# A first stage in an order written out by hand on four engines, weights as a pipeline of half chunks, and batch 1's inputs in room that batch 0 has left

## The chip, the cores and the metric

The kernel runs on one core of one Trainium2 chip. Times are microseconds on the device. A comparison uses the median of several executions; one more execution is profiled, and all rows of a trace below come from that one. TensorE is called PE, VectorE DVE, ScalarE ACT, GpSimd POOL, and SyncE, which issues most of the DMAs, SP.

## What is computed

Three layers follow each other on 8 batches of 576 tokens with 512 channels.

```python
# attention, 8 heads of 64; keys and values are pooled 8 to 1 (72 positions)
k_p = k.reshape(B, H, 72, 8, D).mean(axis=3); v_p = likewise
attn = softmax(q @ k_p^T / 8)
x = attn @ v_p                                  # then heads side by side: (B, 576, 512)
# mixer 1: rank 32 over the tokens, then a channel MLP with 2048 hidden units
u = x + ((x^T @ U) @ V)^T
x = u + relu(u @ w_ch1) @ w_ch2
# mixer 2: real part of a 2-D FFT over tokens and channels, layer norm, channel MLP
u = x + real(fft(fft(x, axis=1), axis=2))
x = u + relu(layernorm(u) @ w_ch1b) @ w_ch2b
```

The weights and U, V arrive as float64 and are turned into float32 on the chip by integer instructions.

## The kernel before

**The long loop.** All 4608 tokens go through both channel MLPs in blocks of 256 tokens. `groups` lists them: the first group takes blocks 0 and 1 together (`wide`), then one block at a time, first for mixer 1, then for mixer 2. In a group a loop runs over the NF = 16 chunks f of 128 hidden units: `st1` makes the hidden chunk (names `h<-uth,w` and `h<-utl,w`), ACT and DVE split it into a high and a low part (`hh`, `hl`, and for odd f of the wide group `hw`; lines 666 and 667), and `st2`, one or two steps later, multiplies it with the second weight (`o`, `h`, `m` `<-w,hh`, `<-w,hl`, `<-w,hw`). Every float32 product is made of three products of high and low parts. Between these, `lanes` (generators stepped by `step`) do the attention of the next batches (`a`), the token mixing (`mix`), the pooling of keys and values (`prep`), the weights (`w`), and later the FFT.

**The first stage.** Before that loop can begin, batch 0 has to pass attention and token mixing. `Attn.prep` loads k and v of a batch (`kT`, `vr`) and pools them on DVE (`kp` L267, `vp` L270). `tile_steps` takes one of five tiles of up to 128 tokens through: scores (`s<-k,q`), the maximum (L334), eight exponentials (L337), transposes (L341, L342), their copy to SBUF (L345, L346), the product with v (`<-v,e`), the division (L358), and the split into `xh` and `xl` (`split`, L98 and L92). `hu_mm` sums the tiles into `hu`. When all five are in, `mix_split` makes `hst` of it, `mix_mm` mixes (`<-hst,vst`) and adds (L95), and `block_prep` transposes and splits into `uth` and `utl` what the loop reads.

**Weights.** A half chunk (weight k of chunk f) is a DMA of 512 KB into `wraw`, then a shift on DVE (L116), an Abs on ACT in place (L117), two bit operations on DVE (L121, L122), a copy on ACT that rounds to the high part (L98), and a subtraction on POOL (L92) for the low part. `w_first` does this for the first weights, both halves of a chunk in one step. Chunks wait in SBUF rooms that are also `scratch` rooms: `scratch(i)` lies where the weight chunk 15 - i // 2 will lie.

**Order.** A scheduler orders the instructions of each engine, from its own model of their times, by priority; `urgent()` raises that of the attention of batch 0. SP's DMAs are issued in one order too, and their packets share the same 16 DMA engines.

Of the kernel before, what the change touches and what calls it, by code (L numbers as in the profile page):

```python
# [8 lines left out]
F32 = mybir.dt.float32  # L9
# [24 lines left out]
GROUPS = ((0,), (1, 2), (3, 4, 5), (6, 7))  # L34
F64_BIAS = float.fromhex("0x1p-112")
# [3 lines left out]
def kernel(  # L39
# [30 lines left out]
    state = {"n": 0, "free": False, "m": "s1", "u": 0, "slot": 0, "x1": 0, "u2": 0}  # L70
# [33 lines left out]
    def urgent():  # L104

        return tc.high_priority(offset=4000)

# [21 lines left out]
    def w_first(tmp):  # L129
        raws, ts = {}, {}  # L130

        def loads(upto):
            while len(raws) < min(NF, upto) and (len(raws) < (NF - 1 if state["free"] else 5) or NF - 2 in ts):
# [4 lines left out]
        def done(f):  # L138
            for k in range(2):
                w = wp.tile([128, 2, 512], F32R, tag=f"w{k}_{f}", name="w")  # L140
                W[k, f] = w
                split(w[:, 0], w[:, 1], ts[f][k].bitcast(F32), nc.gpsimd)
        loads(2)
        yield
        for f in range(NF + 1):
            loads(f + 3)
            while len(raws) < min(NF, f + 1):
                yield
                loads(f + 3)
            if f == NF - 1:  # L150
                done(f - 1)
            if f < NF:
                if f < NF - 2:
                    t = scratch(f % 2)
                    t = [t[:, 512 * k:512 * k + 512].bitcast(I32) for k in range(2)]
                else:
                    t = [tmp().bitcast(I32) for k in range(2)]
                ts[f] = t
                for k in range(2):
                    high(raws[f][k], 512, t[k])  # L160
            yield
            if f and f != NF - 1:
                done(f - 1)
            if f < NF:
                for k in range(2):
                    bits(raws[f][k], 512, t[k])
                yield
# [30 lines left out]
    class Attn:  # L198
# [44 lines left out]
        def prep(self, b):  # L243
# [5 lines left out]
            def load(i):  # L249
                t = scratch(2 + i) if b == 0 else self.tmp()  # L250
# [6 lines left out]
            ahead = 9 if b == 0 else 2  # L257
# [55 lines left out]
        def tile_steps(self, b, t, alt=0, before=None):  # L313
# [11 lines left out]
            if before:  # L325
                before()
            sf = scratch(3 + alt) if alt else p1.tile([128, S], F32, tag="s", name="s")
# [423 lines left out]

    lanes = {}
    at_pool = []

    abx = ExitStack()
    at = Attn(abx)
    at_pool.append(at.p)
# [230 lines left out]
```

## Time and profile before

| | us |
|---|---|
| median of 3 runs (1990.57 to 1992.56) | 1991.53 |
| the profiled execution, its own time | 1994.14 |
| its span, first to last instruction | 1992.4 |
| PE busy in the span | 1925.2 (97%) |
| DVE busy | 837.7 (42%) |
| ACT busy | 534.4 (27%) |
| POOL busy | 213.7 (11%) |

The span holds what the instructions show; the execution's own time has 1.7 us around it. PE's share is an average: it is near the whole of every stretch but the first.

### The profile page before, as it was taken

The numbers are of one execution on the slowest core, as the hardware profiler recorded it, in microseconds if no ns is written. First come the engines' busy times: TensorE is split into PE (matmuls) and PEld (weight loads), VectorE is DVE, ScalarE is ACT, GpSimd is POOL, SyncE is SP. The second block draws the span as 40 slices with busy tenths as digits, with TensorE's granted clock in tenths as the row PEclk, the third lists the DMA queues.
The fourth block names the chain that finished last, engine by engine and source line by source line (L and its number), as shares of the span: only waits on it lengthen the run. The fifth ranks groups of instructions, "written<-read, shape, count | busy, mean of one in ns | idle before, by whom it ended". The sixth has DMA issues, their size and how long they took to land.

```text
span 1992.4 us, 31308 instructions
## 1 busy us (share of the span) xinstructions
PE 1925.2 (97%) x12220; PEld 1712.2 (86%) x12220; DVE 837.7 (42%) x1906; ACT 534.4 (27%) x1709; POOL 213.7 (11%) x323
## 2 busy tenths in 40 slices
PE   5689999999999999999999999999999999999999
PEld 3478888887888888999999899999999999999998
DVE  7984444444453443333334734444433222222221
ACT  6562333332333332122222422212111111111111
POOL 3530000000000000010112511211210000000000
PEclk8699999999999999999999999999999999999999
DMA  9434344435352423242234622322321111101110
GB/s 355 168 101 143 107 132 133 153 114 162 104 156 89 134 86 117 80 138 71 76 93 128 194 69 66 100 84 69 104 70 38 32 38 32 38 32 33 32 33 32
DMA packets 122740, 196.16 MB, mean 98 GB/s; under 512 B 17440, under 2 KB 42112, under 8 KB 122592
## 3 DMA queue, kind: packets, MB, share of 16 engines
q1 hardware_dynamic: 121664, 190.76, 30.5%
q0 software_dynamic: 928, 3.40, 0.5%
q8 instruction: 96, 1.57, 0.3%
q14 instruction: 52, 0.43, 0.1%
HBM read 139.72 MB, written 54.39 MB: 97 GB/s over the span
## 4 chain that ended last, share of the span: by engine, by line
PE 83%; DMA 7%; DVE 6%; issue 2%; POOL 1%; SPq 1%; ACT 0%; DVEq 0%; POOLq 0%; ACTq 0%
PE h L102 37%; PE o L102 36%; PE s L102 6%; DMA raw<-vr 1%; PE m L640 1%; PE hu L102 1%; DMA cv<-w1b 1%; POOL w L92 1%; DMA raw<-kT 1%; DVE scr L121 1%; DVE scr L122 1%; DVE vp L270 1%; DVE scr L116 1%; PE s L341 1%; DMA R<-x1d 1%
## 5 line engine op out<-in xcount | busy, mean ns | idle before, releaser
L102 PE MATMUL h<-uth,w 128*128 128x256 f32 x4608 | 931.0, 284 | 6.3 <-DVE hl L667 4.7
L102 PEld LDWEIGHTS h<-uth,w 128*128 128x128 f32 x4608 | 754.0, 190 | 36.4 <-DVE hl L667 10.0
L102 PE MATMUL o<-w,hh 128*128 128x512 f32 x2208 | 678.1, 398 | 3.1 <-ACT hh L666 3.0
L102 PE MATMUL h<-utl,w 128*128 128x256 f32 x2304 | 652.3, 283 | 0.0
L667 DVE SCALAR_TENSOR_TENSOR hl<-h,hh 128x256 fp32r<-128x256 f32 x560 | 234.2, 420 | 629.9 <-ACT hh L666 628.4
L666 ACT ACTIVATE hh<-h 128x256 fp32r<-128x256 f32 x560 | 214.9, 384 | 996.0 <-PE h L102 939.8
L102 PEld LDWEIGHTS h<-utl,w 128*128 128x128 f32 x2304 | 438.7, 190 | 21.1 <-issue 1.0
L102 PEld LDWEIGHTS o<-w,hh 128*128 128x128 f32 x2208 | 386.2, 189 | 62.0 <-ACT hh L666 4.8
L102 PE MATMUL o<-w,hl 128*128 128x512 f32 x1104 | 411.9, 395 | 0.6 <-DVE hl L667 0.6
L102 PEld LDWEIGHTS o<-w,hl 128*128 128x128 f32 x1104 | 198.6, 189 | 35.4 <-DVE hl L667 1.8
L337 ACT ACTIVATE s<-s,mx 128x72 f32<-128x72 f32 (+1 forms) x296 | 90.0, 326 | 61.6 <-DVE mx L334 61.3
L116 DVE TENSOR_SCALAR cv<-cv 128x256 int32<-128x256 int32 x64 | 18.9, 296 | 126.0 <-DMA cv<-w1b 70.1
L102 PE MATMUL s<-k,q 128*128 128x144 f32 (+1 forms) x296 | 53.4, 306 | 18.7 <-DMA scr<-vr 14.5
L92 DVE TENSOR_TENSOR utl<-m,uth 128x512 fp32r<-128x512 f32 x66 | 45.4, 687 | 55.8 <-ACT uth L98 55.4
L102 PEld LDWEIGHTS s<-v,e 128*128 128x128 f32 (+3 forms) x370 | 55.0, 183 | 15.4 <-issue 11.2
L102 PE MATMUL s<-v,e 128*128 128x192 f32 (+5 forms) x370 | 65.4, 314 | 0.9 <-ACT e L345 0.7
L631 POOL TENSOR_TENSOR rs<-mv,mhalf 128x1 f32<-128x1 f32 x36 | 20.9, 597 | 419.0 <-DVE mv L630 419.0
L102 PEld LDWEIGHTS s<-k,q 128*128 128x128 f32 (+1 forms) x296 | 42.3, 189 | 25.1 <-ACT k L277 14.5
L337 ACT ACTIVATION_READ_ACCUMULATOR s<-s,mx 128x1 f32 (+1 forms) x296 | 62.9, 213 | 0.0
L98 ACT ACTIVATE uth<-m 128x512 fp32r<-128x512 f32 x66 | 39.5, 598 | 75.1 <-PE m L640 75.1
L285 POOL TENSOR_TENSOR v<-vp,vmask 128x128 f32<-128x128 f32 x8 | 3.5, 435 | 506.4 <-PE s L102 495.8
L92 POOL TENSOR_TENSOR w<-scr,w 128x512 fp32r<-128x512 f32 x28 | 43.8, 1574 | 50.6 <-ACT w L98 40.5
(216 smaller groups left out, 1523.7 us busy)
## 6 DMA issues: line engine op xcount, KB each, us to landing
x<-x SPq DMA_DIRECT2D x56, 256.0 KB
ur<-ud SPq DMA_DIRECT2D x36, 256.0 KB
x1d<-ur SPq DMA_DIRECT2D x36, 256.0 KB
ul<-u2d SPq DMA_DIRECT2D x36, 256.0 KB
ur<-u2d SPq DMA_DIRECT2D x36, 256.0 KB
out<-ur SPq DMA_DIRECT2D x36, 256.0 KB
q<-qT SPq DMA_DIRECT2D x32, 256.0 KB
wraw<-w1a SPq DMA_DIRECT2D x16, 512.0 KB
```

Of the source, the lines that this page charges most:

```text
L92: eng.tensor_tensor(out=o, in0=a, in1=b, op=ALU.subtract)
L98: nc.scalar.activation(out=hi, in_=src, func=ACTF.Copy)
L102: nc.tensor.matmul(o, a, b, start=start, stop=stop, skip_group_check=True)
L116: nc.vector.tensor_scalar(out=t, in0=lw, scalar1=29, scalar2=None, op0=ALU.logical_shift_right)
L121: nc.vector.scalar_tensor_tensor(out=t, in0=hw, scalar=-0x80000000, in1=t, op0=ALU.bitwise_and, op1=ALU.bitwise_or)
L122: nc.vector.scalar_tensor_tensor(out=t, in0=lw, scalar=3, in1=t, op0=ALU.logical_shift_left, op1=ALU.bitwise_or)
L270: nc.vector.tensor_reduce(out=vp[:n, i - 4, :], in_=t[:n, 0:512].rearrange("p (s e) -> p s e", e=POOL), op=ALU.add, axis=AX.X)
L337: nc.scalar.activation(out=s[:n, a], in_=v[:, k], func=ACTF.Exp, bias=mx[:n, a:a + 1], accum_out=sm[:n, a:a + 1])
L341: nc.tensor.transpose(e0[:, c * 128:c * 128 + n], sf[:n, c * 128:c * 128 + 128], ident[:n, :n])
L631: nc.gpsimd.tensor_tensor(out=rs[:, 0:1], in0=v, in1=mhalf, op=ALU.pow)
L666: nc.scalar.activation(out=hh, in_=p, func=ACTF.Relu)
L667: nc.vector.scalar_tensor_tensor(out=hl, in0=p, scalar=0.0, in1=hh.bitcast(F32), op0=ALU.max, op1=ALU.subtract)
```

## The change

1. **Written order.** The first stage is built inside `tc.manual_schedule` for PE, ACT, DVE and POOL: their instructions stand in the order in which the code makes them. SP is still ordered by the scheduler. The order is in the string `PLAN`: a letter and a digit is a step of a tile (A scores, B maximum and exponentials, C transposes and copies, D product with v and division, E split, F sum into `hu`), `w` a step of the weights, `u` of U and V, `p` of the pooling, `v` the spread of v. `tile_steps` has two more places to stop for batch 0. `urgent` is gone. After the first stage stands a `no_sync_barrier`, past which nothing is moved to before.
2. **Weights.** `w_first` now steps by half chunks: in one step the third stage of half n-2, the second of half n-1, the first of half n. Until the first stage is over, the rounding copy is on POOL instead of ACT. Loads go ahead five chunks, then seven.
3. **Batch 1's k and v** are loaded all nine ahead into `scratch` rooms, not two ahead into `raw`.
4. In the wide group `mix` and `prep` are stepped once more.

```diff
+PLAN = """A0 A1 A2 w u p B0 p B1 p p p v C0 w D0 B2 E0 A3 C1 w D1 F0 B3 E1 A4 w C2 D2 F1 u B4 E2 C3 w C4 D3 F2 u D4 E3 w F3 E4 F4"""
...
-            while len(raws) < min(NF, upto) and (len(raws) < (NF - 1 if state["free"] else 5) or NF - 2 in ts):
+            while len(raws) < min(NF, upto) and (len(raws) < state["raw"] or (1, NF - 3) in W):
...
+        def done(f, k):
+            w = wp.tile([128, 2, 512], F32R, tag=f"w{k}_{f}", name="w")
+            W[k, f] = w
+            t = ts.pop((f, k)).bitcast(F32)
+            if state["free"]:
+                split(w[:, 0], w[:, 1], t, nc.gpsimd)
+            else:
+                nc.gpsimd.tensor_copy(w[:, 0], t)
+                sub(nc.gpsimd, w[:, 1], t, w[:, 0].bitcast(F32))
+        loads(5)
+        for n in range(2 * NF + 2):
+            yield
+            f, k = divmod(n, 2)
+            if n > 1:
+                done(*divmod(n - 2, 2))
+            if 0 < n <= 2 * NF:
+                g = divmod(n - 1, 2)
+                bits(raws[g[0]][g[1]], 512, ts[g])
+            if n < 2 * NF:
+                loads(f + 6)
...
+                high(raws[f][k], 512, ts[f, k])
...
-                t = scratch(2 + i) if b == 0 else self.tmp()
+                t = scratch(2 + i) if b < 2 else self.tmp()
...
-            ahead = 9 if b == 0 else 2
+            ahead = 9 if b < 2 else 2
...
+        def first(self, plan, do):
+
+            steps = [self.tile_steps(0, t, t % 3) for t in range(5)]
+            for c in plan.split():
+                if c[0] in "ABCDE":
+                    next(steps[int(c[1])])
+                elif c[0] == "F":
+                    t = int(c[1])
+                    self.hu_mm(0, t, *self.done.pop(t))
+                else:
+                    do[c]()
...
+    order = ExitStack()
+    order.enter_context(tc.manual_schedule(engines={getattr(mybir.EngineType, e) for e in ("PE", "Activation", "DVE", "Pool")}))
...
+    at.first(PLAN, {"w": lambda: step("w"), "u": lambda: step("uv"), "p": lambda: next(g, 1), "v": lambda: at.kv_v(0)})
+    del lanes["uv"]
+    state["raw"] = 7
     step("w")
     lanes["prep"] = lane_prep(at)
+    step("prep")
+    at.mix_split(0)
     for t in range(5):
-        with urgent():
-            at.mix_mm(0, t, at.x0[t])
-        if t % 2:
-            step("w")
-        step("prep")
+        at.mix_mm(0, t, at.x0[t])
     state["u"] = S
+    for j in range(2):
+        for _ in block_prep(0, j, at.x0[2 * j:]):
+            pass
     lanes["a"] = lane_a(at)
     lanes["mix"] = lane_mix(at)
...
+    order.close()
+    tc.no_sync_barrier()
+    state["free"], state["raw"] = True, NF - 1
...
-                for name in ("p", "mix", "w", "prep"):
+                for name in ("p", "mix", "w", "prep") + (("mix", "prep") if wide else ()):
```

The rows below are the order of instructions in the two built programs; lines of the change are one to three off those of before (L102 is L103, L98 is L99, L116 is L113, L117 is L114, L121 and L122 are L118 and L119).

**Place one: the queries of tile 3.** SP before, from the last of the ten first weight loads on:

```order
L137 DMA wraw<-w1a 128x1024
L137 DMA wraw<-w2a 128x1024
L252 DMA raw<-kT 128x576 x2
L296 DMA q<-qT 128x4x128
L137 DMA wraw<-w2a 128x1024 x3
```

SP now, from the same load on:

```order
L135 DMA wraw<-w1a 128x1024
L135 DMA wraw<-w2a 128x1024 x3
L294 DMA q<-qT 128x4x128
L250 DMA scr_503<-kT 128x576
L250 DMA scr_505<-kT 128x576
```

The queries of tile 3 stood behind ten weight loads and two of batch 1's k; now they stand behind twelve weight loads.

PE before, where tile 1's product with v (`o_313`), tile 2's transposes (`h_324`) and tile 3's scores (`s_360`) stand:

```order
L102 MATMUL o_313<-v,scr_268 128x64
L102 MATMUL hu<-xh,ust 128x512
L341 MATMUL h_324<-ident,scr_281 128x128 x4
L342 MATMUL h_325<-ident,scr_281 64x128
L102 MATMUL hu<-xl,ust 128x512
L102 MATMUL h_349<-v,scr_331 128x128
L102 MATMUL h_349<-v,scr_331 128x192 x3
L102 MATMUL h_349<-v,scr_331 128x64
L102 MATMUL hu<-scr_321,ust 128x512 x2
L102 MATMUL s_360<-k,q 128x144 x2
L102 MATMUL s_361<-k,q 128x144 x2
```

PE now, from tile 0's product with v (`s_274`) on:

```order
L103 MATMUL s_274<-v,e 128x64
L103 MATMUL s_299<-k,q 128x144 x2
L103 MATMUL s_300<-k,q 128x144 x2
L341 MATMUL o_307<-ident,scr_238 128x128 x4
L342 MATMUL o_308<-ident,scr_238 64x128
L103 MATMUL o_323<-v,scr_314 128x128
L103 MATMUL o_323<-v,scr_314 128x192 x3
```

Tile 3's scores stood behind the products with v of tiles 0 to 2. They now stand right behind tile 0's, ahead of tile 1's transposes (`o_307`).

**Place two: ACT between tile 1 and tile 2**, now. `s_299` are tile 3's scores, `scr_347` is tile 1's split, `h_366` are tile 2's transposes:

```order
L114 ACTIVATE wraw<-wraw 128x512
L337 ACTIVATE s,sm<-s_299,mx 128x72 x4
L337 ACTIVATE s,sm<-s_300,mx 128x72 x4
L99 ACTIVATE scr_347<-scr_329 128x512
L114 ACTIVATE wraw<-wraw 128x512
L345 ACTIVATE scr_373<-h_366 128x512
```

DVE now, over the same steps:

```order
L358 TENSOR_TENSOR scr_329<-o_323,sm 128x512
L334 TENSOR_REDUCE mx<-s_299 128x4
L334 TENSOR_REDUCE mx<-s_300 128x4
L93 TENSOR_TENSOR scr_347<-scr_329,scr_347 128x512
L118 SCALAR_TENSOR_TENSOR scr_271<-wraw,scr_271 128x512
L119 SCALAR_TENSOR_TENSOR scr_271<-wraw,scr_271 128x512
L113 TENSOR_SCALAR scr_363<-wraw 128x512
L347 TENSOR_SCALAR sm<-sm 128x8
L348 RECIPROCAL sm<-sm 128x8
L358 TENSOR_TENSOR scr_384<-h_378,sm 128x512
```

Before, the scheduler had put between such steps whatever instruction of the weights its model held to be ready; now one step of a half chunk stands between two tiles, and the Abs of a half chunk (L114) stands ahead of the next tile's copy.

**Place three: DVE where the loop begins.** Before, from the last split of the first stage to the first split of the loop (`h_593`):

```order
L92 TENSOR_TENSOR utl<-s_586,uth 128x4x128
L122 SCALAR_TENSOR_TENSOR scr_774<-wraw,scr_774 128x512
L334 TENSOR_REDUCE mx<-s_899 128x4
L116 TENSOR_SCALAR scr_840<-wraw 128x512
L270 TENSOR_REDUCE vp<-raw 128x64
L121 SCALAR_TENSOR_TENSOR scr_840<-wraw,scr_840 128x512
L270 TENSOR_REDUCE vp<-raw 64x64
L122 SCALAR_TENSOR_TENSOR scr_840<-wraw,scr_840 128x512
L667 SCALAR_TENSOR_TENSOR hl<-h_593,hh 128x256
```

DVE now, over the same place (`scr_476` is chunk 2, `scr_591` chunk 3; the first split of the loop follows these rows and reads `h_601`):

```order
L93 TENSOR_TENSOR utl<-s_569,uth 128x4x128
L118 SCALAR_TENSOR_TENSOR scr_476<-wraw,scr_476 128x512
L113 TENSOR_SCALAR scr_591<-wraw 128x512 x2
L265 TENSOR_REDUCE kp<-scr_503 128x72
L265 TENSOR_REDUCE kp<-scr_505 128x72
L265 TENSOR_REDUCE kp<-scr_507 128x72
L265 TENSOR_REDUCE kp<-scr_509 128x72
L268 TENSOR_REDUCE vp<-scr_511 128x64
L268 TENSOR_REDUCE vp<-scr_513 128x64
```

Before, chunks 0 to 6 and 14 were through DVE's part of the conversion at this place and part of chunk 7 too, and seven of batch 1's nine poolings. Now chunks 0 and 1 and half of chunk 2 are, and none of the poolings.

## Rows read from the trace of the kernel before

**Rows 1.** The page: busy tenths of PE and DVE in 40 slices of the span, and the granted clock in tenths.

```profile
PE   5689999999999999999999999999999999999999
...
DVE  7984444444453443333334734444433222222221
...
PEclk8699999999999999999999999999999999999999
```

**Rows 2.** Stretches of the span: length, then busy time and count of PE, PEld, DVE, ACT and POOL, the granted clock, the DMA engines' share and GB/s.

```profile
0.00:32.00 32.00, 12.18 (x62) 9.57 (x63) 21.48 (x47) 18.18 (x73) 8.03 (x17) 0.99 0.97 341
13.40:82.40 69.00, 41.81 (x152) 30.08 (x153) 65.86 (x116) 44.26 (x145) 32.75 (x24) 0.63 0.73 264
14.00:31.00 17.00, 11.91 (x61) 9.29 (x61) 16.47 (x38) 15.43 (x68) 3.98 (x6) 1.00 1.03 389
31.00:85.50 54.50, 33.01 (x105) 23.89 (x106) 50.66 (x78) 29.95 (x85) 30.04 (x20) 0.50 0.66 231
82.40:131.20 48.80, 41.64 (x245) 34.51 (x245) 47.34 (x80) 31.33 (x102) 19.19 (x15) 0.96 0.44 147
131.20:165.00 33.80, 33.47 (x209) 28.15 (x208) 18.95 (x44) 14.45 (x49) 7.91 (x9) 1.00 0.42 134
```

**Rows 3.** PE in order of time: start, duration, instruction, and in brackets the idle time before it and what ended it.

```profile
14.47 2.29 PE L102 MATMUL s<-k,q 128*128 128x144 f32 x8 [14.47 <-DMA scr<-vr]
...
21.96 1.80 PE L102 MATMUL s<-v,e 128*128 128x128 f32 x10
...
31.73 3.33 PE L102 MATMUL h<-v,scr 128*128 128x128 f32 x10 [1.72 <-ACT scr L345]
...
37.74 2.12 PE L102 MATMUL s<-k,q 128*128 128x144 f32 x8
...
44.64 1.05 PE L341 MATMUL s<-ident,s 128*128 128x128 f32 x4
...
61.70 0.79 PE L102 MATMUL hu<-scr,ust 64*128 64x512 f32 x1 [0.75 <-DVE scr L92]
70.77 0.80 PE L102 MATMUL o<-hst,vst 128*128 128x512 f32 x1 [8.27 <-DVE hst L92]
...
78.06 1.06 PE L640 MATMUL s<-ident,scr 128*128 128x128 f32 x4
...
81.92 0.58 PE L102 MATMUL h<-uth,w 128*128 128x256 f32 x1
...
143.62 0.40 PE L102 MATMUL h<-w,hw 128*128 128x512 f32 x1
```

**Rows 4.** SP in order of time: the last first weight load, batch 1's k, and the queries of tile 3.

```profile
19.92 0.33 SPq L137 DMA_DIRECT2D wraw<-w2a  x1
21.19 1.62 SPq L252 DMA_DIRECT2D raw<-kT  x2
23.83 0.38 SPq L296 DMA_DIRECT2D q<-qT  x1
```

**Rows 5.** ACT in order of time: a copy of transposes, a split, the first and the last two of eight exponentials of a tile, and an Abs.

```profile
31.02 0.65 ACT L345 ACTIVATE scr<-h 128x512 f32<-128x512 f32 x1
...
39.60 0.63 ACT L98 ACTIVATE scr<-scr 128x512 fp32r<-128x512 f32 x1 [2.77 <-DVE scr L358]
...
42.50 0.30 ACT L337 ACTIVATE s<-s,mx 128x72 f32<-128x72 f32 x1
...
44.56 0.35 ACT L337 ACTIVATE s<-s,mx 128x72 f32<-128x72 f32 x1
44.77 0.24 ACT L337 ACTIVATION_READ_ACCUMULATOR s<-s,mx 128x1 f32 x1
...
51.90 0.71 ACT L117 ACTIVATE wraw<-wraw 128x512 f32<-128x512 f32 x1 [0.42 <-DVE cv L116]
```

**Rows 6.** DVE in order of time: the division of tile 0, the two maxima of a tile, the division of tile 4, the split of `hst`, the last split of the first stage, and a split of chunk 5 in the loop.

```profile
24.73 0.67 DVE L358 TENSOR_TENSOR scr<-s,sm 128x512 f32<-128x512 f32 x1
...
41.41 0.81 DVE L334 TENSOR_REDUCE mx<-s 128x4 f32<-128x288 f32 x2
...
58.78 0.67 DVE L358 TENSOR_TENSOR scr<-o,sm 64x512 f32<-64x512 f32 x1
...
70.02 0.69 DVE L92 TENSOR_TENSOR hst<-hu,hst 32x512 fp32r<-32x512 f32 x1
...
81.79 0.67 DVE L92 TENSOR_TENSOR utl<-s,uth 128x512 fp32r<-128x512 f32 x1
...
139.84 0.42 DVE L667 SCALAR_TENSOR_TENSOR hw<-h,hw 128x256 fp32r<-128x256 f32 x1
```

**Rows 7.** DVE from 82.4 to 131.2 us by line and shape: count, busy time and mean ns of one, idle time before.

```profile
L121 DVE SCALAR_TENSOR_TENSOR scr<-wraw,scr 128x512 int32<-128x512 int32 x13 | 13.0, 1011 | 0.0
L122 DVE SCALAR_TENSOR_TENSOR scr<-wraw,scr 128x512 int32<-128x512 int32 x14 | 10.3, 750 | 0.0
L116 DVE TENSOR_SCALAR scr<-wraw 128x512 int32<-128x512 int32 x13 | 8.5, 687 | 1.2 <-DMA wraw<-w1a 1.2
L270 DVE TENSOR_REDUCE vp<-raw 128x64 f32<-128x512 f32 x5 | 3.3, 674 | 0.2 <-DMA raw<-vr 0.2
...
L267 DVE TENSOR_REDUCE kp<-raw 128x72 f32<-128x576 f32 x4 | 2.9, 736 | 0.0
...
L122 DVE SCALAR_TENSOR_TENSOR cv<-wraw,cv 128x512 int32<-128x512 int32 x1 | 0.7, 678 | 0.0
...
L116 DVE TENSOR_SCALAR cv<-wraw 128x512 int32<-128x512 int32 x1 | 0.4, 375 | 0.0
```

**Rows 8.** A bit operation on DVE and the subtraction that POOL ran at that time, each from its engine's timeline.

```profile
125.94 1.67 DVE L121 SCALAR_TENSOR_TENSOR cv<-wraw,cv 128x512 int32<-128x512 int32 x1
...
125.77 1.29 POOL L92 TENSOR_TENSOR w<-scr,w 128x512 fp32r<-128x512 f32 x1 [1.34 <-ACT w L98]
```

More of the change, by code (lines that the diff above doesn't have):

```diff
@@ L69 @@
     W = {}
-    state = {"n": 0, "free": False, "m": "s1", "u": 0, "slot": 0, "x1": 0, "u2": 0}
+    state = {"n": 0, "free": False, "m": "s1", "u": 0, "slot": 0, "x1": 0, "u2": 0, "raw": 5}
     def scratch(i, w=1024, dt=F32):
@@ L137, in loads @@
                     nc.sync.dma_start(out=raws[f][k], in_=(w1a, w2a)[k][f].bitcast(I32))
[L138 to L152, printed above, removed]
+        def done(f, k):
[18 more added lines that the diff above has]
+                loads(f + 6)
+                while len(raws) <= f:
+                    yield
+                    loads(f + 6)
                 if f < NF - 2:
-                    t = scratch(f % 2)
-                    t = [t[:, 512 * k:512 * k + 512].bitcast(I32) for k in range(2)]
-                else:
[L157 to L167, printed above, removed]
+                    if not k:
+                        t = scratch(f % 2)
+                        ts[f, 0], ts[f, 1] = [t[:, 512 * i:512 * i + 512].bitcast(I32) for i in range(2)]
+                else:
+                    ts[f, k] = tmp().bitcast(I32)
+                high(raws[f][k], 512, ts[f, k])
     def w_second(tmp):
@@ L370, in tile_steps @@
             yield
-        def first(self):
-            todo = list(range(5))
-            act = []
-            while todo or act:
-                if todo and len(act) < 3:
-                    t = todo.pop(0)
-                    act.append((t, self.tile_steps(0, t, t % 3)))
-                with urgent():
-                    for t, g in list(act):
-                        if next(g, 1):
-                            act.remove((t, g))
-                            self.hu_mm(0, t, *self.done.pop(t))
-                yield
+        def first(self, plan, do):
[8 more added lines that the diff above has]
+                    do[c]()
         def tiles(self, b):
@@ L764 @@
     at.kv_k(0)
-    for _ in g:
-        pass
     lanes["w"] = w_first(at.cv)
     lanes["uv"] = at.setup_uv()
-    f = at.first()
-    next(f)
-    at.kv_v(0)
-    for _ in f:
-        step("uv")
-        step("w")
-    with urgent():
-        at.mix_split(0)
+    at.first(PLAN, {"w": lambda: step("w"), "u": lambda: step("uv"), "p": lambda: next(g, 1), "v": lambda: at.kv_v(0)})
+    del lanes["uv"]
+    state["raw"] = 7
     step("w")
     lanes["prep"] = lane_prep(at)
+    step("prep")
+    at.mix_split(0)
     for t in range(5):
-        with urgent():
-            at.mix_mm(0, t, at.x0[t])
-        if t % 2:
-            step("w")
-        step("prep")
+        at.mix_mm(0, t, at.x0[t])
     state["u"] = S
+    for j in range(2):
+        for _ in block_prep(0, j, at.x0[2 * j:]):
+            pass
     lanes["a"] = lane_a(at)
     lanes["mix"] = lane_mix(at)
-    for j in range(2):
-        g = block_prep(0, j, at.x0[2 * j:])
-        more = True
-        while more:
-            with urgent():
-                more = not next(g, 1)
-            if more:
-                step("w")
-    state["free"] = True
+    order.close()
+    tc.no_sync_barrier()
+    state["free"], state["raw"] = True, NF - 1
     hq = []
```

7 lines of the change are left out of this document (4 added, 3 removed).

## The prediction

> **What bounds the kernel now.** I read the page first [rows 1]: PE is at nine tenths or more from the third slice on, and only the first two slices (100 us) show idle PE and a lowered clock. So the change can move the time only through the state in which PE enters the long loop. Then the stretches [rows 2]: from 131.2 us on PE is busy 33.47 of 33.80 us at the full clock while DVE is busy 18.95, so there PE sets the pace. Before that it is DVE: 65.86 of 69.0 us between 13.4 and 82.4, and 47.34 of 48.8 until 131.2. The reader is to see that PE does not begin the loop when it is free but when DVE is through (first loop matmul at 81.92 [rows 3]), and that for another 49 us PE is fed by a DVE that never rests. Last, PE's own timeline: it waits 14.47 us for the first loads and 8.27 us for `hst`, and the product with v takes 1.80 us at 22 us but 3.33 us at 32 us [rows 3]. The granted clock stands behind that: 1.00 until 31 us, that is 2.4 GHz, then 0.50 (1.2 GHz) until 85.5 [rows 2], after PE had been busy 11.91 of 17 us; it comes back once the loop runs densely.
>
> So the measure is: DVE's total work up to the point where it stops being the bound is nearly the same in both kernels, since every half chunk needs its three DVE instructions. What the change can give or take is (a) idle time of DVE inside the first stage and (b) how far DVE's work is along when PE enters the loop.
>
> **The first stage, walked through in the new order.** Until tile 0's division little differs: about 24.7 us, as in [rows 6].
>
> Tile 1. PE's next instructions are tile 3's scores. Their queries were issued at 23.83 us behind ten weight loads of 512 KB and two of k of 288 KB [rows 4]; now twelve weight loads stand ahead. Summed from the sizes, some 10.5 MB are then ahead or in it, instead of 10.0. At the mean 341 GB/s of the first 32 us [rows 2] that is 30.7 us; with a microsecond for the last packets I take 32. PE idles from 25 to 32, and tile 1's transposes, which stand behind, idle with it. PE has then worked less than before up to 31 us, so I take the lower clock from there on: scores 2.1, transposes 1.1, product 3.3 [rows 3], with a copy of 0.7 [rows 5] and the division of 0.7 [rows 6] between and behind them: 32 + 2.1 + 1.1 + 0.7 + 3.3 + 0.7 = 39.9 us.
>
> Tile 2. The division is followed by tile 3's maximum (0.4 for one half [rows 6]), its eight exponentials (42.50 to 44.9, 2.4 us [rows 5]), and only then, on ACT, by tile 1's split (0.6), for whose result DVE waits (0.7). DVE then does the two bit operations of a half chunk (0.6 each from start to start) and a shift (0.4), ACT the Abs (0.7) that stands ahead of tile 2's copy (0.7), PE the product (3.3), DVE the division (0.7): 11.1 us, so 51.0. Tile 3 likewise, with half of V (2.1 us by its smaller shapes) in place of the half chunk and without the split: 2.1 + 0.4 + 2.4 + 0.6 + 0.7 + 3.3 + 0.7 = 10.2, so 61.2. Tile 4's product only follows on PE (two sums into `hu` at 0.79 each [rows 3], 0.6 from start to start, product 3.0): 65.4.
>
> To `hst`: split 0.7, bits 1.2, shift 0.4, Abs 0.7, split 1.3, again bits 1.2, shift 0.4, Abs 0.7, `hst` 1.2: 73.2 us (70.71 before [rows 6]). From there 81.92 - 70.71 = 11.2 us passed before; seven conversion and pooling instructions, about 5.5 us, lay between and are gone, so the loop begins at about **79** and the last split ends at about **80** us (82.4 before). The first stage is hardly shorter. DVE's own work in it is 31.5 us by undisturbed prices (0.6 for 512 elements, 0.34 for a shift), in 66.5 us: some 35 us of DVE idle, where before there were 3.
>
> **The loop's beginning.** Before, DVE entered with chunks 0 to 6 and 14 done and seven of batch 1's nine poolings; now with two and a half chunks and no pooling. To the split of chunk 5's second half (139.84 us before [rows 6]) DVE's new order has 120 instructions. In the stretch 82.4 to 131.2 it did 80, of much the same mix (43 of 80 on weights, 68 of 120 now; the rest poolings, maxima, splits), in 47.34 us [rows 2]; weighted by kind 120 cost 73 us, and with the 1.5 us idle of that stretch 74.5. So that split ends at 80 + 74.5 = **154.5**. What reads it began at 143.62 [rows 3]; now it can begin no sooner than 154.5: 10.9 us late. In the new order PE has by then done one more product with v and one pair of transposes, about 1.4 us of work that would come later: 9.5 us. From here on PE set the pace before [rows 2], and as DVE is then past chunk 11 it does so again; I see nothing later that gives the 9.5 us back.
>
> **The other edits.** POOL's four copies have no row. From below, a single small POOL instruction is free where POOL is idle; from above each costs the 1.29 us of a subtraction [rows 8]. POOL is busy 32.75 of 69 us [rows 2] and nothing in the loop needs chunk 0 before 79 us: 0 to 5 us that lie under the tiles' chain, taken as 0; without that cover the 5 us would stand ahead of the loop. ACT loses four copies of 0.6 us and waits anyway: 0. Batch 1's nine loads (2.3 MB, 6 us at 389 GB/s) run while the DMA engines are at 0.66 [rows 2]; the last waits for tile 4's room (about 70 us) and is needed at 86: 0. If it came late, the poolings would hold up all of DVE behind them, microsecond for microsecond. The additional steps of `mix` and `prep` move work between 150 and 200 us, where PE never waits: 0, with a microsecond either way. Loads of chunks 7 to 13 start only when the first stage has left their rooms (about 78 us); 14 loads at 389 GB/s end near 98 us, ahead of DVE's use of chunk 7 at about 110: 0.
>
> **DVE against POOL.** In [rows 7] the same bit operation takes 1011 ns where an undisturbed one takes 678, and [rows 8] shows one: 1.67 us, begun 0.17 us after a subtraction of 1.29 us on POOL. Undisturbed (0.34 for a shift, 0.60 for a bit operation, the others' means in [rows 7] less the 0.07 by which one overlaps the next) the 80 instructions make 37.2 us, so 10.1 us went to this over 13 subtractions, 0.8 us each. The new sum has this loss in it by rows. The Trainium skill (SBUF — State Buffer, § SBUF: two separate sides) says that an instruction of DVE in a two-port mode, or with two SBUF inputs against a POOL instruction that reads SBUF, and POOL exclude each other, and the later one is blocked for the whole instruction. The row at 125.94 agrees (1.29 - 0.17 + 0.6 is 1.7); taken for each of the 24 subtractions until 154 us, by the rows' 1.29 us, it would add 24 x 0.5 = 12 us, the slower rival below.
>
> **Rivals.**
> - *Faster: the queries of tile 3 land before PE needs them.* If they are there by 25 us, PE does not idle and the clock may stay at its upper level: 6 us of waiting are gone, and products of 1.8 instead of 3.3, scores and transposes at half take some 9 us off tiles 1 to 4 and the mixing. The loop begins at 64 us, the 10.9 becomes -4, the time 1986. For: the clock was 1.00 until 31 us. Against: the load order. It decides from a landing before about 28 us.
> - *No change: the clock stays up, or the disturbances shrink.* The clock alone gives 9 us, or half of DVE's loss in the loop disappears because POOL's subtractions meet poolings, which the single-input rows (674, 736 ns) show undisturbed: 73 becomes 65 us. Either makes 1992 to 1993.
> - *Slower still.* POOL holds DVE up for the whole of each subtraction, not 0.8 us of it: 12 us as above, 2013. Or PE, which until 131 us was busy 41.64 of 48.8 [rows 2] and now waits more, falls to 1.2 GHz in the loop too: matmuls at twice the price for some 12 us of them, the same.
>
> **Numbers.** The sum stands against the profiled execution: span 1992.4, own time 1994.14, which is 2.6 above the median of the runs. 1991.5 + 9.5 = 2001 for the median. Chances: forecast 0.45, slower still 0.14, no change 0.19, faster 0.22. What a measurement can tell from no change is 0.2%, 4 us: faster 0.22, same 0.19, slower 0.59. Walked waits of four tiles can be off by 5 us either way, so the likeliest case alone is 1996 to 2007; with the other cases 1984 to 2013.
>
> **What would show it.** Tile 3's scores (L103, `s<-k,q`) near 32 us with a wait of some 6 us for a DMA ahead of them; divisions (L358) near 40, 51, 61 and 65; DVE idle some 35 us before 80, on ACT (L99, L345) and PE; the first `h<-uth,w` at 79; the clock at 0.50 from 31 to 80; DVE above 95% until 150, PE waiting on `hl` and `hw` (L667); the split of chunk 5 at 154. The prediction is wrong if the divisions come 5 us apart, if the loop starts before 70, or if DVE is through its 120 instructions in under 62 us.

## The result, and the profile after

The changed kernel takes 2017.16 us (median of 4 runs, 2016.18 to 2018.12), the kernel before 1991.79 beside it: 1.0128 times as long (95% interval 1.0110 to 1.0145), 25 us slower. The forecast was 2001 with 1984 to 2013 around it: slower was right, the size was not. The profiled execution took 2017.82 us with a span of 2016.0.

The page, three lines of the changed kernel, as in [rows 1]:

```profile
PE   3679999999999999999999999999999999999999
...
DVE  3897245344444344323334644344343322222221
...
PEclk8789999999999999999999999999999999999999
```

DVE now stands at 3 in the first slice (50 us), where it was at 7, and at 8 and 9 in the second and third. Stretches of the changed kernel, columns as in [rows 2]:

```profile
13.40:80.80 67.40, 38.62 (x150) 29.74 (x151) 34.96 (x72) 28.00 (x115) 10.34 (x14) 0.70 0.54 186
80.80:160.50 79.70, 59.52 (x316) 48.40 (x314) 78.35 (x122) 46.10 (x141) 36.97 (x27) 0.87 0.46 161
90.00:100.00 10.00, 7.85 (x37) 6.76 (x37) 10.00 (x17) 6.35 (x24) 5.59 (x5) 0.70 1.03 410
130.00:140.00 10.00, 5.61 (x20) 4.05 (x20) 10.00 (x17) 4.34 (x14) 4.27 (x3) 0.68 0.36 100
```

From the start of the weights to the loop DVE is busy 34.96 of 67.4 us, where it was busy 65.86 of 69.0 [rows 2]. Then it does not rest for 80 us, and PE, which reached 41.64 of 48.8 us there, has 59.52 of 79.7. The granted clock falls again in parts of the loop: to 0.70 and 0.68 in the last two rows, in which PE is busy 7.85 and 5.61 of 10 us.

PE in order of time, changed kernel, as in [rows 3]:

```profile
32.83 2.26 PE L103 MATMUL s<-k,q 128*128 128x144 f32 x8 [9.86 <-DMA q<-qT]
...
36.63 2.49 PE L103 MATMUL o<-v,scr 128*128 128x128 f32 x10 [0.47 <-ACT scr L345]
...
46.98 3.33 PE L103 MATMUL h<-v,scr 128*128 128x128 f32 x10 [5.19 <-ACT scr L345]
...
73.78 0.79 PE L103 MATMUL o<-hst,vst 128*128 128x512 f32 x1 [2.77 <-DVE hst L93]
...
80.35 0.36 PE L103 MATMUL h<-uth,w 128*128 128x256 f32 x1 [0.93 <-DVE utl L93]
...
160.59 0.38 PE L103 MATMUL h<-uth,w 128*128 128x256 f32 x1
...
163.56 0.40 PE L103 MATMUL h<-w,hw 128*128 128x512 f32 x1
```

And DVE: the five divisions, and the split of chunk 5's second half, as in [rows 6]:

```profile
23.01 0.69 DVE L358 TENSOR_TENSOR scr<-s,sm 128x512 f32<-128x512 f32 x1 [2.71 <-PE s L103]
...
39.16 0.69 DVE L358 TENSOR_TENSOR scr<-o,sm 128x512 f32<-128x512 f32 x1 [9.29 <-PE o L103]
...
50.35 0.69 DVE L358 TENSOR_TENSOR scr<-h,sm 128x512 f32<-128x512 f32 x1 [3.87 <-PE h L103]
...
60.77 0.69 DVE L358 TENSOR_TENSOR scr<-s,sm 128x512 f32<-128x512 f32 x1 [0.52 <-PE s L103]
...
64.86 0.68 DVE L358 TENSOR_TENSOR scr<-o,sm 64x512 f32<-64x512 f32 x1 [1.17 <-PE o L103]
...
160.13 0.41 DVE L667 SCALAR_TENSOR_TENSOR hw<-h,hw 128x256 fp32r<-128x256 f32 x1
```

Tile 3's scores wait 9.86 us for their queries, and tile 1's transposes and product stand behind them on PE, so DVE idles 9.29 us ahead of tile 1's division. What DVE waits for between 20 and 80 us (line, for what; us in total, times, longest):

```profile
DVE scr L358 <- PE o L103: 10.5, 2, 9.3
DVE scr L93 <- ACT scr L99: 6.9, 3, 2.8
DVE scr L358 <- PE h L103: 3.9, 1, 3.9
```

The middle line is the splits of tiles; two of the three waits are for an ACT half that stands behind another tile's exponentials.

In the loop, the start of each chunk's first matmul against before shows where the time goes: chunk 0 comes 1.6 us earlier, chunk 1 is 4.0 late, chunk 2 11.0, chunk 4 12.8, chunk 6 19.8, chunk 8 22.1, chunk 12 22.2. From chunk 8 on PE sets the pace again, and nothing is given back. The span ends 23.6 us later.

### The profile page after: what moved, and what is told of

It reads as the page before. It is cut to its first block, busy times and chain, and to the rows that moved or that the text cites. A ratio compares the mean times of both kernels' runs of the same rounds, so it can differ in the third digit from the quotient of the medians.

```text
span 2016.0 us, 31343 instructions
## 1 busy us (share of the span) xinstructions
PE 1930.7 (96%) x12220; PEld 1719.3 (85%) x12220; DVE 836.7 (42%) x1906; ACT 534.0 (26%) x1705; POOL 213.9 (11%) x327
## 4 chain that ended last, share of the span: by engine, by line
PE 81%; DMA 7%; DVE 3%; issue 1%; ACT 1%; SPq 0%; POOL 0%; DVEq 0%; POOLq 0%; ACTq 0%
PE h L103 36%; PE o L103 35%; PE s L103 6%; DMA raw<-vr 2%; PE m L640 1%; PE hu L103 1%; DMA ul<-ud 1%; DMA ud<-x 1%; DMA cv<-w2b 1%; PE s L341 1%; DMA cv<-w1b 1%; DMA raw<-kT 0%; DVE vp L268 0%; DMA R<-x1d 0%; DMA x1d<-ur 0%
## 5 line engine op out<-in xcount | busy, mean ns | idle before, releaser
L103 PE MATMUL h<-uth,w 128*128 128x256 f32 x4608 | 931.8, 285 | 8.9 <-DVE hw L667 4.6
L103 PEld LDWEIGHTS h<-uth,w 128*128 128x128 f32 x4608 | 754.6, 191 | 37.6 <-DVE hw L667 6.1
L103 PE MATMUL o<-w,hh 128*128 128x512 f32 x2208 | 678.5, 398 | 2.9 <-ACT hh L666 2.9
L103 PE MATMUL h<-utl,w 128*128 128x256 f32 x2304 | 652.2, 283 | 0.0
L103 PEld LDWEIGHTS h<-utl,w 128*128 128x128 f32 x2304 | 439.3, 191 | 20.3 <-issue 0.4
L103 PEld LDWEIGHTS o<-w,hh 128*128 128x128 f32 x2208 | 387.1, 189 | 63.9 <-issue 4.2
L103 PE MATMUL o<-w,hl 128*128 128x512 f32 x1104 | 410.5, 395 | 2.9 <-DVE hl L667 2.9
L103 PEld LDWEIGHTS o<-w,hl 128*128 128x128 f32 x1104 | 198.2, 189 | 36.6 <-DVE hl L667 3.1
L103 PE MATMUL s<-k,q 128*128 128x144 f32 (+1 forms) x296 | 53.6, 303 | 25.2 <-ACT k L275 14.3
L113 DVE TENSOR_SCALAR cv<-cv 128x256 int32<-128x256 int32 x64 | 18.8, 294 | 135.4 <-DMA cv<-w2b 74.8
L103 PEld LDWEIGHTS s<-v,e 128*128 128x128 f32 (+3 forms) x370 | 56.0, 185 | 17.7 <-issue 10.8
L103 PE MATMUL s<-v,e 128*128 128x192 f32 (+5 forms) x370 | 66.8, 317 | 2.7 <-ACT e L346 2.1
L103 PEld LDWEIGHTS s<-k,q 128*128 128x128 f32 (+1 forms) x296 | 42.3, 187 | 31.4 <-ACT k L275 14.7
L99 ACT ACTIVATE uth<-m 128x512 fp32r<-128x512 f32 x66 | 39.5, 599 | 74.5 <-PE m L640 74.4
L96 DVE TENSOR_TENSOR ur<-o,ur 128x512 f32<-128x512 f32 x70 | 46.2, 685 | 4.8 <-PE o L103 3.4
```

Source lines behind the costliest of these rows:

```text
L96: eng.tensor_tensor(out=o, in0=a, in1=b, op=ALU.add)
L99: nc.scalar.activation(out=hi, in_=src, func=ACTF.Copy)
L103: nc.tensor.matmul(o, a, b, start=start, stop=stop, skip_group_check=True)
L113: nc.vector.tensor_scalar(out=t, in0=lw, scalar1=29, scalar2=None, op0=ALU.logical_shift_right)
```

## Experiments

Each ratio is to the kernel before, run beside it. In the expectations theory A is that DVE's idle time in the written first stage is the cost, since DVE bounds until the last of the first weights is converted; theory B (in two runs C) stands for the rival of that run. The kernel before lay between 1990.2 and 1992.1 us beside these runs, so a difference of two times that has no ratio can be off by 2 us. In the loop the scheduler orders every one of these kernels anew, so an edit there also changes the order of DVE's other instructions.

**Undo the written order alone.** The scheduler orders again, batch 0's attention at its old priority, and the barrier behind the first stage goes with the order; all other parts stay:

```diff
-    order.enter_context(tc.manual_schedule(engines=...))
...
-                    next(steps[int(c[1])])
+                    with urgent():
+                        next(steps[int(c[1])])
```

> The changed kernel with its written order taken away: the scheduler orders all engines again, with the attention of batch 0 at the priority that it had before; half chunks, batch 1's loads and the additional steps stay. Theory A (the written order leaves DVE idle in the first stage, 44.5 us of it until the last first weight is converted, against 17.9 before, and what is idle there comes back as delay because DVE bounds until then): idle falls to 15 to 25 us, the last conversion comes at 140 to 150 us, the time is 1990 to 1998. Theory B (the half chunks, the poolings of batch 1 in a burst or the additional steps cost it): the time stays at 2008 or above whatever DVE's idle time.

1994.1 us, 1.0021 (1.0011 to 1.0030): some 4 us above the kernel before, where the changed kernel is 25 above it. So about 21 of the 25 us are the written order's, its barrier included; the two were not undone one by one. The same stretch, from the start to the end of DVE's last bit operation on the first weights, in both kernels and here (columns as above). Before:

```profile
0.00:140.90 140.90, 93.16 (x454) 72.84 (x455) 122.97 (x212) 82.27 (x267) 59.16 (x51) 0.81 0.62 216
```

The changed kernel:

```profile
0.00:176.30 176.30, 113.39 (x552) 89.96 (x553) 131.81 (x226) 85.83 (x284) 60.31 (x59) 0.83 0.54 182
```

The changed kernel in the scheduler's order:

```profile
0.00:140.00 140.00, 92.75 (x462) 73.19 (x462) 122.76 (x212) 82.05 (x267) 62.23 (x55) 0.84 0.63 217
```

DVE idle: 17.9, 44.5 and 17.2 us. With DVE's idle time back where it was, the end of the conversions is too, and the time all but 4 us.

**Undo parts 3 and 4; and do them alone in the kernel before.**

```diff
-                t = scratch(2 + i) if b < 2 else self.tmp()
+                t = scratch(2 + i) if b < 1 else self.tmp()
...
-                for name in ("p", "mix", "w", "prep") + (("mix", "prep") if wide else ()):
+                for name in ("p", "mix", "w", "prep"):
```

> The changed kernel with batch 1's k and v loaded two ahead again and without the additional steps of mix and prep; written order and half chunks stay. Theory A: these parts move DVE's work within the stretch in which it bounds, the time stays within 4 us of 2017. Theory B (nine poolings in a burst where the loop begins hold up the splits): 2009 or less, and the first splits of the loop 4 us or more earlier than 90.5.

> The kernel before with batch 1's k and v loaded nine ahead and the additional steps of mix and prep; its order and its weights stay. Theory A: within 4 us of the kernel before (1988 to 1996). Theory B: 2000 or more.

Alone in the kernel before: 1990.4 us, 1.0002 (0.9993 to 1.0012), as A had it. Out of the changed kernel: 2029.1 us, 1.0196 (1.0181 to 1.0211): neither theory. Early it looks like B (chunk 4 begins at 123.6, not 138.2), but batch 1's tokens, which block 2 needs, are late: its mixing still runs on PE at 218 to 222 us, and from the first group's last chunk to block 2's first 21.9 us go by, not 8.0. Both kernels from 220 to 240 us; without parts 3 and 4:

```profile
220.00:240.00 20.00, 15.91 (x79) 12.07 (x78) 7.16 (x16) 8.10 (x34) 0.00 (x0) 0.91 0.33 100
```

With them:

```profile
220.00:240.00 20.00, 19.31 (x125) 16.98 (x125) 7.99 (x16) 5.83 (x18) 0.00 (x0) 1.00 0.29 90
```

So the two parts, which I had costed at 0, save the written order another 12 us.

**Other plans.** Four more strings in the changed kernel: tile 3's scores behind tile 1's division; six more weight steps in the waits (the plan has twelve `w` where the changed kernel has six; the expectation says five); two that also take tiles closer together, convert U and V early and then allow seven chunks (`r`). In this order:

```diff
-PLAN = "... v C0 w D0 B2 E0 A3 C1 w D1 F0 B3 E1 A4 w C2 D2 F1 u B4 E2 C3 w C4 D3 F2 u D4 E3 w F3 E4 F4"
+PLAN = "... v C0 w D0 B2 E0 C1 w D1 A3 F0 B3 E1 A4 w C2 D2 ..."
+PLAN = "... v C0 w D0 B2 w E0 A3 C1 w w w D1 F0 B3 w E1 A4 w C2 w D2 F1 u B4 w E2 ..."
+PLAN = "... v C0 w u D0 B2 w E0 C1 w D1 E1 u r C2 w F0 D2 E2 w A3 F1 A4 B3 w F2 w B4 C3 w w D3 E3 C4 w F3 D4 E4 w F4"
+PLAN = "... v C0 w u D0 B2 w E0 C1 w D1 E1 A3 u r C2 B3 w D2 F0 E2 C3 A4 w D3 B4 F1 E3 F2 w C4 w D4 F3 w E4 w F4"
```

> One edit in the plan: tile 3's scores (A3) stand behind tile 1's division (D1) instead of ahead of its transposes, so tile 1 no longer waits for the queries of tile 3. Theory A (the loop is late because DVE idles in the first stage and then sets the pace): tile 1's division comes some 8 us earlier, near 31 us instead of 39, the loop begins near 72 instead of 79, and the whole time falls by as much: 2009 to 2012. Theory B (what counts is the state of the weights and the clock in the loop, not when the loop begins): the loop begins earlier but the time stays within 3 us of 2017, since DVE and PE then wait for something else.

> Five more steps of the weights stand in the plan, each at a place where DVE waited in the changed kernel (behind the maxima and behind the copies); nothing else is moved. At the loop's beginning five more half chunks are through DVE. Theory A: each takes about 1.55 us of undisturbed DVE work, 2 us with the disturbance by POOL, off a loop that DVE bounds: 2005 to 2009, with the loop beginning within 2 us of 79. Theory B (PE's lowered clock in the loop is the bound): under 4 us of gain.

> The changed kernel with another plan: tiles 1 and 2 go through ahead of tile 3's scores, U and V are converted early, then chunks 5 and 6 may be loaded, twelve steps of the weights stand between the tiles. By theory A: divisions near 24, 32, 38, 48 and 52, the loop begins near 66 (62 to 70) with six and a half chunks past DVE instead of two and a half, DVE idle until the last conversion 20 to 28 us; against before the loop begins 16 us earlier with 8 us less weight work and 5 us less pooling done: 1989 (1983 to 1997). If idle DVE isn't the cause (theory B): 2008 or more.

> The changed kernel with a plan that mends what the run with tiles close together showed (tile 3's scores and exponentials waited behind weight steps, two weight steps stood ahead of the end): tile 3's scores ahead of tile 2's copy, ten weight steps, none twice in a row. If the order of the steps is the cause: divisions near 23, 32, 40, 46 and 52, the loop begins at 62 to 68, chunk 12 at 0 to 9 us behind the kernel before, time 1993 to 2002. If any written order has this cost: 2006 or more.

| kernel | us | loop begins | DVE idle until last conversion | chunk 12 against before |
|---|---|---|---|---|
| before | 1991.8 | 81.9 | 17.9 | 0 |
| scheduler's order | 1994.1 | 81.5 | 17.2 | -1.8 |
| tiles closer still | 2006.0 | 72.8 | 28.8 | +12.8 |
| tiles close together | 2006.2 | 78.2 | 31.1 | +16.0 |
| weights in waits | 2012.6 | 82.3 | 34.5 | +17.7 |
| scores of tile 3 later | 2014.3 | 74.9 | 38.3 | +18.5 |
| changed | 2017.2 | 80.4 | 44.5 | +22.2 |

All four gained less than A asked for. The run with later scores, 2.8 us faster than the changed kernel, even stays within the 3 us that B had given it, and the closer plan lies at the rival's bound; the other two fit neither theory. Yet all four stand in A's order: the delay at chunk 12 goes with DVE's idle time, some 0.8 to 1.2 us for each microsecond over the 17.9, and not with the start of the loop (a kernel that begins it 9 us earlier than the one before is 15 us slower). The idle time is counted up to the last conversion, whose own end it shifts, so that column is a tally of where DVE's time went and not a cause set from outside. The weight steps in the waits were partly without work: the program allowed only five chunks to be loaded by then. In the plan with tiles close together a second cause shows on PE's timeline:

```profile
46.91 0.27 PE L342 MATMUL s<-ident,s 128*64 128x128 f32 x1
53.72 3.33 PE L103 MATMUL s<-v,e 128*128 128x128 f32 x10 [6.54 <-ACT e L345]
```

Tile 3's copy stood on ACT behind tile 4's exponentials, these waited for a maximum, and that stood on DVE behind two weight steps. The closer plan mends this, but still leaves 11.6 us more idle than the scheduler's order; at 2006.0 it ends at the very edge that I had given to "any written order has this cost". No plan of mine reached the scheduler's; that none can is not shown.

**The price of DVE's time.** Twenty subtractions that nobody reads in the kernel before; and the loop's bit operations left out of the changed kernel:

```diff
+            for _ in range(5 if b == 0 and t < 4 else 0):
+                sub(nc.vector, dummy[:n], xh[:n, 0:384].bitcast(F32), xl[:n, 0:384].bitcast(F32))
```

```diff
     def bits(raw, n, t):
...
+        if state["free"] and n == 512:
+            return t.bitcast(F32)
```

> The kernel before with 20 additional subtractions of 128x384 on DVE, five behind the split of each of tiles 0 to 3, into a room that nobody reads: about 0.48 us each, 9.6 us of DVE time between 28 us and 85 us, and nothing else changed. Theory A (until the last first weight is converted DVE's time is the time): 8 to 13 us slower than before, 2000 to 2005, the last conversion 8 to 13 us later than 140.9. Rival (something else sets the start of the loop, and PE makes up for it there): less than 4 us slower.

> The changed kernel with the two bit operations of a half chunk left out where the half chunk is converted in the loop (the weights of these chunks are then wrong, the shift, the Abs, the copy and the subtraction stay); the first stage is untouched. Theory A (DVE bounds the first eight chunks of the loop, the lowered clock there is its consequence): some 26 x 1.35 = 35 us less on DVE, PE at its full pace soon after 80 us, chunk 8 begins 25 to 37 us earlier than 177.2, time 1980 to 1992. Rival (the lowered clock and PE's own chains bound there): chunk 8 less than 12 us earlier, time 2005 or more.

With more work: 1996.2 us, 1.0025 (1.0016 to 1.0034), 4.7 us slower; the last conversion ends 7.2 us later, chunk 8 begins 7.4 later. A had 8 to 13, the rival under 4: it fell between them. The twenty took 0.55 us each, up to 1.6 where POOL subtracted, some 13 us in all: DVE's time counts, at about half its length by chunk 8 and a third at the end. Without bit operations: 1997.0 us, 20 less than the changed kernel (A asked for 25 or more, the rival for 12 or less), chunk 8 at 155.9, 21 us earlier; the mechanism of A with less than its size. Two stretches of this run:

```profile
80.00:100.00 20.00, 14.22 (x72) 11.59 (x71) 14.01 (x28) 15.73 (x43) 13.88 (x15) 0.86 1.00 396
100.00:120.00 20.00, 17.24 (x108) 14.57 (x106) 15.08 (x26) 17.07 (x52) 14.02 (x11) 0.97 0.44 129
```

DVE now has slack, and PE is still short of full; ACT, at 17.07 of 20 us, may be the next to hold it up, which no run tests. The granted clock recovers with PE's work (0.97 from 100 us on, and 1.00 from 120), so its fall in the loop of the changed kernel goes back to the waits. It can't have made the split of chunk 5 late: up to there DVE is busy 78.35 of 79.7 us, so waiting for PE at whatever clock took at most the 1.4 us between. At chunk 12 this run is level with the kernel before (0.2 us earlier), and yet its span ends 4.1 us later: from 300 to 500 us PE is busy 191.5 us at a granted clock of 0.97, before 194.7 at 1.00. So what follows chunk 12 isn't the same in all kernels either.

**POOL in DVE's way.** In the first two runs ACT makes a second copy in place of POOL's subtraction (in the changed kernel for the half chunks of the loop, in the kernel before for all of them), so that the correction by the low part of those weights is left out. In the other three DVE subtracts, in the loop or, in the last, everywhere, and all work is kept:

```diff
-                split(w[:, 0], w[:, 1], t, nc.gpsimd)
+                split2(w[:, 0], w[:, 1], t)
```

```diff
-                split(w[:, 0], w[:, 1], t, nc.gpsimd)
+                split(w[:, 0], w[:, 1], t, nc.vector)
```

> The changed kernel, with POOL's subtraction of a half chunk in the loop replaced by a second copy on ACT: the low part then holds the rounded weight itself, which leaves the correction out of the computation. DVE's instructions stay. Theory A with the disturbance as a cause: between 80.8 and 160 us DVE lost some 20 us to POOL; without it DVE is through chunk 5 near 141 instead of 160 and the time falls to 1998 to 2003. Theory C (the disturbance is not what makes it late; PE and ACT are): less than 6 us of gain.

> The same replacement in the kernel before, for all half chunks; the correction is left out of the computation here too. Theory A: DVE lost 23 us to POOL until 142 us, 12 of them ahead of the loop; the loop begins near 70 to 74 and the time falls by 8 to 14 us, to 1978 to 1984, less than the changed kernel gains by it. Theory C: within 4 us of before.

> The kernel before with the subtraction that makes a half chunk's low part on DVE instead of POOL where the half chunk is converted in the loop; all work is kept. Some 15 half chunks: 15 x 0.6 = 9.3 us more on DVE, which at the price of the run with 20 additional subtractions (4.7 us for 10.9) costs 4 to 6 us. If POOL's work stands in DVE's way (the run without it gained 11.6): 1984 to 1988. If that gain came from the work left out: 1996 to 1998.

> The same in the changed kernel, some 27 half chunks: 16 us more on DVE, 9 us by the price of the run without bit operations (20 us for 35). If POOL stands in DVE's way (15 us): 2008 to 2013. If not: 2022 to 2028.

> The kernel before with this subtraction on DVE throughout, in the first stage too, where DVE is busy 65.9 of 69 us and POOL 32.8. If POOL stands in DVE's way there too (0.8 us of each subtraction against 0.6 us of additional work): 1981 to 1987, the loop's first matmul no later than 81.92. If not: 1998 or more, the loop 8 us later.

Without POOL's subtraction: 2002.0 (15 us less) in the changed kernel and 1980.4 (11.6 less) before, both times as expected; but in the former the split of chunk 5 came at 149.4 us, not near 141, with 140 DVE instructions to it in place of 121. On DVE: 2004.5 in the changed kernel, 12.6 us less although DVE has one instruction more for each half chunk; 1989.1 before, 0.9986 (0.9977 to 0.9996); 1989.1 before with all of them, 0.9992 (0.9981 to 1.0003). In the changed kernel the gain is larger than I expected. In the kernel before it is 2 us where I expected 3 to 7, and with all subtractions moved, where I expected 4 to 10, none that stands clear of the noise, although the loop begins at 74.9. But each of the three is far from the loss that I had given for POOL not being in the way (5 us or more). DVE by line and shape, changed kernel, 80.8 to 160.6 us, columns as in [rows 7]:

```profile
L118 DVE SCALAR_TENSOR_TENSOR scr<-wraw,scr 128x512 int32<-128x512 int32 x21 | 18.9, 925 | 0.0
L119 DVE SCALAR_TENSOR_TENSOR scr<-wraw,scr 128x512 int32<-128x512 int32 x21 | 17.8, 867 | 0.0
L113 DVE TENSOR_SCALAR scr<-wraw 128x512 int32<-128x512 int32 x21 | 12.6, 635 | 0.0
L93 DVE TENSOR_TENSOR xl<-x,xh 128x512 fp32r<-128x512 f32 x3 | 3.1, 1033 | 0.0
L347 DVE TENSOR_SCALAR sm<-sm 128x8 f32<-128x8 f32 x4 | 2.8, 706 | 0.0
L265 DVE TENSOR_REDUCE kp<-scr 128x72 f32<-128x576 f32 x4 | 2.7, 736 | 0.0
...
L119 DVE SCALAR_TENSOR_TENSOR cv<-wraw,cv 128x512 int32<-128x512 int32 x2 | 2.5, 1230 | 0.0
L667 DVE SCALAR_TENSOR_TENSOR hw<-h,hw 128x256 fp32r<-128x256 f32 x6 | 2.5, 409 | 0.0
...
L118 DVE SCALAR_TENSOR_TENSOR cv<-wraw,cv 128x512 int32<-128x512 int32 x2 | 2.4, 1214 | 0.0
...
L113 DVE TENSOR_SCALAR cv<-wraw 128x512 int32<-128x512 int32 x2 | 1.9, 939 | 0.0
```

The same with the subtraction on DVE, 100 to 150 us, where POOL does nothing:

```profile
L93 DVE TENSOR_TENSOR w<-scr,w 128x512 fp32r<-128x512 f32 x16 | 11.0, 687 | 0.0
L118 DVE SCALAR_TENSOR_TENSOR scr<-wraw,scr 128x512 int32<-128x512 int32 x16 | 10.8, 690 | 0.0
L119 DVE SCALAR_TENSOR_TENSOR scr<-wraw,scr 128x512 int32<-128x512 int32 x15 | 10.3, 691 | 0.0
L113 DVE TENSOR_SCALAR scr<-wraw 128x512 int32<-128x512 int32 x14 | 5.3, 422 | 0.0
L93 DVE TENSOR_TENSOR xl<-x,xh 128x512 fp32r<-128x512 f32 x4 | 2.8, 690 | 0.0
...
L265 DVE TENSOR_REDUCE kp<-raw 128x72 f32<-128x576 f32 x3 | 2.2, 746 | 0.0
L667 DVE SCALAR_TENSOR_TENSOR hw<-h,hw 128x256 fp32r<-128x256 f32 x5 | 2.1, 414 | 0.0
...
L347 DVE TENSOR_SCALAR sm<-sm 128x8 f32<-128x8 f32 x3 | 0.5, 168 | 0.0
```

Bit operations lose 235 and 176 ns on average, the shift 213, the split with two SBUF inputs 343, and a scaling of 8 columns takes 706 ns in place of 168. Poolings (one input) and splits that read PSUM (`hw`) lose nothing (736 to 738 and 409 ns; in the second run 746 and 414). The Trainium skill (SBUF — State Buffer, § SBUF: two separate sides) says that DVE and POOL exclude each other where DVE runs in a two-port mode, or has two SBUF inputs while POOL reads SBUF, and that DVE's own ports wait for nobody. The rows agree on the forms with two SBUF inputs and on those untouched; that the shift and the scaling with one input run in such a mode is what the rule would ask for, no run here tests it. That the changed kernel gained 12.6 us although its last conversion ended only some 4 us earlier (begun at 171.4 us, not 175.6) shows that the waits of PE on single splits matter beside DVE's sum. Part of this is the new order: to the split of chunk 5's second half, which begins at 143.76 us in place of 160.13, DVE has 60 instructions on weights besides its 20 subtractions, where the changed kernel has 68. How POOL's disturbance and the order divide the 12.6 us stays open.

**Can both be beaten?** Two more: the scheduler's order with weights converted only three chunks ahead, and the kernel before with parts 3 and 4 and the subtraction on DVE.

```diff
-            while ph == 0 and (1, min(f + 2, NF - 1)) not in W:
+            while ph == 0 and (1, min(f + (3 if wide else 2), NF - 1)) not in W:
...
+                    if name != "w" or not wide or second:
+                        step(name)
```

> The kernel of the scheduler's order (half chunks and batch 1's loads kept, no written order) with the weights in the wide group converted only as the loop needs them, three chunks ahead, not two half chunks a step. Theory A: DVE has the same work, but less of it stands ahead of the splits that PE waits for between 80 and 140 us, where PE is idle 5.7 us in the scheduler's order: 1987 to 1992. Rival: the conversions come later and meet batch 1's attention, the waits only move: 1994 or more.

> The kernel before with batch 1's loads nine ahead, the additional steps of mix and prep, and the subtraction of a half chunk on DVE in the loop. The first two moved nothing (1.0002), the last gave 0.14%: 1986 to 1990, if the gains add. If the earlier poolings now stand ahead of the splits on a DVE that does the subtraction as well: 1992 or more.

1994.8 us (1.0016) and 1996.6 us (1.0027, 1.0016 to 1.0039), as the rivals had it: no gain in the first, and in the second the gains don't add, it is 6 us slower. What is left is the kernel before with the loop's subtraction on DVE, 2 us faster than before, less than the 0.2% that I count as a difference.

## Why the prediction was right and wrong

**Right: the first stage.** The scores of tile 3 near 32 us (32.83), divisions done at 39.9, 51.0, 61.2 and 65.4 (39.85, 51.04, 61.46, 65.54), `hst` at 73.2 (its split ended at 73.7), the loop at 79 (80.35), some 35 us of DVE idle (32.4 between 13.4 and 80.8). The wait for the queries was 9.9 us, not 6 to 7, since tile 0 was done earlier. The clock was mixed (0.65 on average from 31 to 80 us), not 0.50 throughout. That the first division fits so closely is in part luck: the queries came 0.8 us later than forecast, and tile 1's product took 2.49 us in place of 3.3.

**Right: which term it is.** DVE bounds in the loop until 160 us, PE waits for `hl` and `hw`, and nothing later gives it back.

**Wrong: the size of the carry-over,** "What reads it began at 143.62 [rows 3]; now it can begin no sooner than 154.5: 10.9 us late". It began at 163.56, 19.9 late. The step that failed is this carry-over: the work of DVE in the loop was priced too low, and its end was set against the wrong instant. Three parts make up the difference to the 9.5 that went into the sum:
- The reader doesn't follow the split at once, neither before nor now. Before, the split ended at 140.26 and the reader came 3.4 us later, since PE made the hidden part of chunk 6 between; now they are 160.54 and 163.56, with the same 24 matmuls between (160.59 to 163.56). I compared the new split with the old reader. Split against split 154.5 would have been 14.2 late: 3.4 us of the miss, and the 1.4 us that I took off for work of PE done by then were never given back: the lag is 19.8 us at chunk 6 and 22.1 at chunk 8.
- DVE took 79.7 us for the 121 instructions to that split (the row's 122 has one more that begins within it), not 74.5: 5.2 us. By the prices of the run with the subtraction on DVE the rows above lose some 19 us, about 0.9 for each of 22 subtractions; I had 0.8. The instructions of the conversions cost nearly what scaling by kind had carried over: 0.80 us each on average before [rows 7, 8] and 0.82 now, 1.3 us in all. What it missed is other forms that POOL also holds up. In the stretch of [rows 7] the split with two SBUF inputs and the scaling had met no subtraction (675 and 154 ns, the rows below); now three such splits took 1033 ns on average and four such scalings 706, 3.3 us more than at the old prices. The remaining 0.6 us is not divided further.
- The stretch began 0.8 us later than 80.

The two forms in the kernel before, in the view and stretch of [rows 7]:

```profile
L92 DVE TENSOR_TENSOR xl<-x,xh 128x512 fp32r<-128x512 f32 x2 | 1.4, 675 | 0.0
...
L347 DVE TENSOR_SCALAR sm<-sm 128x8 f32<-128x8 f32 x3 | 0.5, 154 | 0.0
```

3.4 + 1.4 + 5.2 + 0.8 = 10.8, against 19.9 - 9.5 = 10.4 (the reader now follows its split 0.4 us sooner than before). Another 2 us are lost by chunk 8, since DVE still bounded, and 1.4 between chunk 12 and the end.

**The rivals.** The faster one fell with the landing of the queries at 32.8. No change fell because the clock stayed low (0.65) and the loss for each subtraction did not shrink. The slower one, with POOL holding DVE for the whole of each subtraction, gave 2013 and was nearer in time but not by its mechanism: the loss stayed at about 0.9 of 1.29 us. The clock did fall in the loop, as the other half of that rival had it, but DVE had only 1.4 us of idle time in the stretch that set the delay.

**The other edits.** POOL's copies at nothing: they took 0.68 us each under the tiles' chain, and all of parts 2 to 4 together come to 0.21% in the scheduler's order. Parts 3 and 4 at 0: right in the kernel before (1.0002), wrong in the written order, where they save 12 us.

## What to carry to other kernels

When one engine bounds up to some point in the program, count its idle time up to that point: an order that shortens a chain of tiles but leaves this engine waiting moves its work behind the start, where it is paid for. Compare like with like when a delay is carried along, the producer with the producer. When a loss by contention is carried to a longer stretch, price it for every form that can be held up, also those that happened to meet no disturbance in the rows at hand. A scheduler's order that looks mixed may be filling waits that a written order has to fill by hand.

## What the runs showed of the hardware that was not expected

That a subtraction costs less on the engine that is the bottleneck: taken from POOL to DVE it adds 0.69 us to DVE for each half chunk, and the changed kernel is 12.6 us faster (part of which may be DVE's new order; in the kernel before the same move gave 2 us). And that a tiny instruction can be held up like a large one: of the four scalings of 128x8 values in the changed kernel's stretch, two took 1.25 us or a little more while POOL subtracted (at 121.15 and 154.95 us) and two 0.16 us; in the run where POOL idled they took 0.17 us.
